# Earlier requests for w_out pieces, six buffers for turned output squares, and two queues for the third last output

## The chip, the core and the metric

The kernel runs on one NeuronCore of a Trainium2 chip. The core has a matmul engine (TensorE, PE in the profile; its weight loads are listed as PEld), VectorE (DVE), ScalarE (ACT), GpSimd (POOL) and SyncE (SP). The engines run side by side, each through its own list of instructions in a fixed order, and wait for one another through semaphores. Transfers between the memory outside (DRAM) and the memory on the chip (SBUF) are issued by an engine, here SP and, at the very end, ACT too. Results of PE land in the banks of PSUM[...].

The metric is the device time of one execution in microseconds (us), median of several runs; lower is better.

## What is computed

A causal attention with a decay for each head and without a softmax, and behind it a feed-forward layer with a squared ReLU:

```python
scores = scale * np.matmul(q, k.transpose(0, 1, 3, 2))     # q, k, v: (8, 8, 576, 64)
ret = scores * Dmat                                        # gamma[h] ** (i - j), 0 above the diagonal
attn = np.matmul(ret, v)
x = attn.transpose(0, 2, 1, 3).reshape(4608, 512)
h = np.maximum(x @ w_in, 0.0)                              # w_in: (512, 2048)
out = (h * h) @ w_out                                      # w_out: (2048, 512)
```

The two weights arrive as 64-bit floats[...]: the kernel turns them into 32-bit floats itself, by integer work on the two halves of each word.

## The kernel before

**Three stages.** The 4608 tokens are nine blocks of 512. While the attention of later tokens is computed, 128 tokens at a time, the first product (x @ w_in) of the blocks already there runs between. Then block 8's first product ends, and last comes the second product (with w_out), which runs over `N_K` = 42 outer products k, seven for each of six column sets of 384.

Both feed-forward products are made by Strassen's scheme with seven products instead of eight (`PRODUCTS`); the second uses it twice, an outer and an inner one. Block 0's first product alone is a plain one (`first_in`), since w_in is still being converted then.

**The first product, blocks 1 to 8.** `ffn_in(n, mp, j)` is one step: product j of 0 to 6 in group mp of 0 to 3 of block n. In the loop around it, `whole(i)` does the attention of 128 tokens, `loads(i)` asks for coming q, k and v, and `ffn(i - 1)` runs seven steps: a group of seven products follows every attention part. The products of a group go to three PSUM banks: h_a (j = 0 and 3), h_b (1, 4 and 6), h_c (2 and 5). Product 0 is copied by ACT (L727), 1 and 2 are added to that by DVE (L729, L731), 3 goes through ACT (L733, squared at L735), and 4, 5 and 6 are added by DVE (L736, L740, L743), each with a squaring behind it (L724). A product that adds into a bank waits until the reading of the one before it has ended. In block 1, steps 1 to 4 of the first three groups also make the four sums of w_in for the group that follows (`sum_w_in`, L257 to L260). ACT copies the running attention state out of PSUM at L503 (u_sb <- u_ps); PE's L570 adds to u_ps again.

**Converting w_out beside it.** `w_out_parts` is a generator of small actions on DVE. For each of 16 pieces: L227 (exponent bits), L231 with ACT's L235 beside it, L238, L241 and L244; after every second piece the sums of w_out (L264 to L267), and now and then a store of finished parts. A piece is asked for by `fetch_w` (L214), in four transfers on SP. The first three are actions of the generator; the others are put into the list `transfers` when the buffer they go to has been used up. How many actions a step takes is decided by `late_w2`, the number of actions that should have been done by now less `n_w2`, the number done: it begins after eight steps of block 1, takes an action whenever the number is above zero (two at j = 0 or 3 if it is above 1.5), and none in the steps that turn k and q for the attention (`busy`). `step()` runs one step and then issues one waiting transfer, or two where more than two wait, unless the attention is due within two steps (`QUIET`).

SP's order of work near the start of block 1 is: two stores of block 0's last squares (L691, the second waiting for ACT's square at L687), three stores of block 1's first group (L650), the loads of q, k and v (L158, L156), two more stores, the twelve transfers of the first three pieces (L214), and so on.

**The output.** The rows of a finished part are turned on DVE in squares of 32 by 32 (`leave`, L1036) into one of three buffers in `room` (`t_room`), used in turn, and stored from there by transfers of 32 partitions (L1043), each waiting for its own part. A store goes to the queues given in `queues` in turn: SP alone, except for the last two outer products, which `last_inner` sends out in five smaller parts over SP and ACT. The other outputs are put into the list `leaving` by `outer(k)` and leave one outer product later. The third last output is that of k = `N_K - 3`.

Of the kernel before, what the change touches and what calls it, by code (L numbers as in the profile page):

```python
# [41 lines left out]
def kernel(  # L42
# [33 lines left out]
    nc = tc.nc  # L76
# [12 lines left out]
    N_BLK = n_tok // TOK  # L89
# [39 lines left out]
    room = const.tile([128, 15872], F32, name="room")  # L129
# [36 lines left out]
    N_W1 = N_DF  # L166
# [9 lines left out]
    def raw_of(j):  # L176
        return raw_all[j % N_RAW] if j < N_W1 else raw_all[(j - N_W1) % 3]
# [27 lines left out]
    def fetch_w(j):  # L205
        if j < len(pieces) and wide:
            to = raw_of(j).bitcast(I64)
            if pieces[j][0] == 0:
                nc.sync.dma_start(to.rearrange("p (c f) -> p c f", c=N_DM), piece_src(j))
                return  # L210
            to = to.rearrange("p (o s b c) -> o s p b c", o=2, s=2, b=4)
            for o in range(2):
                for s in range(2):
                    nc.sync.dma_start(to[o, s], piece_src(j)[o, s])  # L214
# [53 lines left out]

    def w_out_parts():

        for j in range(N_W1, N_W1 + 3):
            yield lambda j=j: fetch_w(j)
        for j in range(N_W1 + 1, len(pieces), 2):

            assert not [t for t in transfers if t[0] == N_BLK]
            pair = [round_parts(j - 1), round_parts(j)]
            for one, two, beside, *_ in pair:
                yield one
                yield two, beside
            for i, (_, _, _, three, four, five) in zip((j - 1, j), pair):  # L280
                yield three
                yield four

                def last(i=i, five=five):
                    five()
                    transfers.append((N_BLK, lambda: fetch_w(i + 3)))

                yield last
            wi, m, e = pieces[j]
            mh, mq = divmod(m, N_MQ)  # L290
            if e == 1:

                at = slice(2 * mh, 2 * mh + 2)
                b = [stage[0][:, o, at, :] for o in range(4)] + [stage[1][:, o, at, :] for o in range(3)]
                r1, r2, r3, r4 = right_sums(*b)
                yield from (r1, r2, r3, r4)
            if e == 1 and mh == 1:

                def keep(o):
                    nc.sync.dma_start(w2_dram[o, :, mq, :], stage[o // 4][:, o % 4, :, :].rearrange("p s f -> p (s f)"))  # L300

                yield from right_sums(*(stage[0][:, :, o, :] for o in range(NP)))
                for o, r in enumerate(right_sums(*(stage[1][:, :, o, :] for o in range(NP)))):
                    yield lambda o=o, r=r: [r(), keep(o)]
                yield [lambda: [keep(4), keep(5)]]
                yield [lambda: keep(6)]
# [48 lines left out]
    for half in range(2):  # L355
        at = slice(CH * half, CH * half + CH)
# [345 lines left out]
    def ffn_in(n, mp, j):  # L702

        if j == 0 and mp == 0:

            if n not in sums_x:
                sums_x[n] = sum_x(n)
            for f in sums_x[n]:
                f()
        left, right, to = PRODUCTS[j]  # L710
        if j in OPENS:
            sums[to] = ps_f.tile([128, 2, HT], F32, tag="f", name=f"h_{to}")
        p = sums[to]
        for mm in range(2):
            w = w_in[mp][:, mm, WI_SLOT[left], :, :]
            for c in range(2):
                nc.tensor.matmul(p[:, mm, :], lhsT=w[:, c, :], rhs=xs[n][right][:, c, :],  # L717
                                 start=(j in OPENS and mm == 0 and c == 0), stop=(j in CLOSES and c == 1),
                                 skip_group_check=True)
        g = g_of(mp)  # L720
        p1, u2, p15 = (p_room[mp % 2][:, s, :, :] for s in range(3))

        def square(t):
            nc.vector.scalar_tensor_tensor(t, t, 0.0, t, op0=ALU.max, op1=ALU.mult)  # L724

        if j == 0:
            nc.scalar.copy(p1, p)  # L727
        elif j == 1:
            nc.vector.tensor_tensor(u2, p, p1, op=ALU.add)  # L729
        elif j == 2:  # L730
            nc.vector.tensor_tensor(p15, p, p1, op=ALU.add)  # L731
        elif j == 3:
            nc.scalar.activation(g["A11"], p, AF.Relu)  # L733
        elif j == 4:
            nc.scalar.activation(g["A11"], g["A11"], AF.Square)  # L735
            nc.vector.tensor_tensor(g["A22"], p, p15, op=ALU.add)  # L736
            square(g["A22"])
        elif j == 5:

            nc.vector.tensor_tensor(g["S3"], p, u2, op=ALU.add)  # L740
            square(g["S3"])
        else:
            nc.vector.tensor_tensor(g["A12"], p, p1, op=ALU.add)  # L743
            square(g["A12"])
            queue.extend(g_sums(n, mp))

        if j == 5:
            g_store(n, mp, "A11")
            transfers.append((n, lambda: g_store(n, mp, "A22")))

        if mp == N_MP - 1 and j in (3, 4, 5) and n_next[0] > n + 1:
            if n + 1 not in sums_x:
                sums_x[n + 1] = sum_x(n + 1)
            sums_x[n + 1].pop(0)()
        if j in (6, 0, 1, 2, 3):
            some(2 if n == 1 and mp == 0 else 1)
        if n == 1 and 1 <= j < 5 and mp + 1 < N_MP:
            sums_w.setdefault(mp + 1, sum_w_in(mp + 1)).pop(0)()

        late_w2 = 0.96 * (done[0] - N_0 - 8) - n_w2[0]  # L760
        count = 0 if busy[0] else 2 if late_w2 > 1.5 and j in (0, 3) else late_w2 > 0
        while w_out_next[0] and (count or type(w_out_next[0]) is list):
            f = w_out_next[0]
            if held[0] and type(f) is tuple or ahead[0] <= QUIET and type(f) is list:
                break
            n_w2[0] += 1
            count -= type(f) is not list
            w_out_next[0] = next(w_out_steps, None)
            for f in f if type(f) in (tuple, list) else (f,):
                f()  # L770
            if type(w_out_next[0]) is list:
                break
        if n == N_BLK - 2 and mp == 3 and j in (0, 3):
            assert w_out_next[0] is None
            fetch_w2(j // 3)

    steps = []
    w_out_steps = w_out_parts()  # L780
    w_out_next = [next(w_out_steps)]
    held = [False]
    ahead = [N_DF]
    transfers = []
    busy = [False]
    n_w2 = [0]

# [21 lines left out]
    N_0 = N_W1  # L809
    done = [0]  # L810
# [130 lines left out]
    TC = 3 * HT // 2  # L941
    NQ = TC // 2
    N_K = N_BLK * HT // TC * NP
# [3 lines left out]
    A_room = [late.tile([128, size], F32, name=f"a{j}") for j in range(2)] + [room[:, at:at + size] for at in (5888, 11776)]  # L947
    s_room = [late.tile([128, N_M * NQ], F32, name="s0"), room[:, 10240:10240 + N_M * NQ]]
    O_ = [room[:, at:at + 2 * TC].rearrange("p (e t) -> p e t", e=2) for at in (0, 2 * TC, 4 * TC)]
    t_room = [room[:, at:at + 2 * TC].rearrange("p (a e c) -> p a e c", e=2, c=32) for at in (2304, 3072, 3840)]  # L950
    LOW, HIGH = slice(0, N_MQ), slice(N_MQ, N_M)
    LEFT, RIGHT = slice(0, NQ), slice(NQ, TC)

# [70 lines left out]
    leaving = []  # L1024
    n_left = [0]
# [4 lines left out]

    def leave(k, o, h, e, es, lo, hi, queues=(nc.sync,)):

        t = t_room[n_left[0] % 3]
        n_left[0] += 1
        to, at = t[:, 0:(hi - lo) // 32, es, :], o[:, es, lo:hi]
        nc.vector.transpose(to.rearrange("p a e c -> p e a c"), at.rearrange("p e (a c) -> p e a c", c=32))  # L1036
        for b, at, c, w in runs(k // NP, lo, hi):
            row = b * TOK + h * HT + at
            to = out[row:row + w, e * HT:(e + 1) * HT].rearrange("(a r) (p e c) -> p r a e c", r=32, e=2, c=32)[:, :, :, es, :]
            lo_ = (c - lo) // 32  # L1040
            for p in range(4):
                own = slice(32 * p, 32 * p + 32)
                queues[p % len(queues)].dma_start(to[p], t[own, lo_:lo_ + w // 32, es, :])  # L1043
# [61 lines left out]
    def outer(k):  # L1105

        n, j = divmod(k, NP)
        r = state.pop(k)["r"]
        if k >= N_K - 2:
            return  # L1110
        X, Y, Z = XYZ(k)
        for to, x, with_ in {2: [(Z, r, X), (Y, Y, Z)], 3: [(X, r, X)], 4: [(Z, r, Z), (X, r, Y)], 5: [(Z, r, Z)],
                             6: [(Y, r, Y)]}.get(j, []):
            nc.vector.tensor_tensor(to, x, with_, op=ALU.add)
        if j >= 3:
            o, h, e = {3: (X, 0, 0), 4: (X, 1, 1), 5: (Z, 1, 0), 6: (Y, 0, 1)}[j]
            leaving.append(lambda: leave(k, o, h, e, slice(0, 2), 0, TC))


    n_last = 0  # L1120
# [17 lines left out]
    for k in range(N_K + 1):  # L1138
        j = k % NP
# [81 lines left out]
```

## Time and profile before

| | us |
|---|---|
| median of three runs | 937.07 (936.6 to 937.17) |
| the profiled execution, whole | 939.68 |
| its span, from the first to the last instruction | 937.6 |
| mean granted clock of PE | 0.995 |

The profile comes from one execution. Busy times are shares of its span; a timeline gives for each instruction its start, its length, engine, line, operation, result and operands, and in brackets how long the engine had stood idle and what ended that. The granted clock is the share of PE's full clock that the throttle let through in a stretch.

PE's busy share and granted clock in 40 equal slices of the span:

```profile
PE   8999989999999999999999999999999999999997
...
PEclk9999989999999999999999999999999999999999
```

### The profile page before, as it was taken

How to read it: one execution, taken by the hardware profiler on the slowest of the kernel's cores; microseconds unless marked ns; L12 is line 12 of the kernel's file. 1: busy time of each engine (PE TensorE's matmuls, PEld its weight loads, DVE VectorE, ACT ScalarE, POOL GpSimd, SP SyncE). 2: the span in 40 equal slices, each digit the busy share in tenths (PEclk: the TensorE clock that was granted, in tenths of full speed). 3: DMA queues.
4: the chain of work that ended last, by engine and by line, in shares of the span. 5: the costliest groups of instructions: out<-in, count | busy, mean ns of one | idle time of the engine just before them, and what ended most of it. 6: DMA issues, size and time to landing. Idle time of an engine off the chain costs nothing.

```text
span 937.6 us, 21090 instructions
## 1 busy us (share of the span) xinstructions
PE 925.9 (99%) x8548; PEld 832.7 (89%) x8548; DVE 760.3 (81%) x1215; ACT 346.0 (37%) x788; POOL 80.3 (9%) x82
## 2 busy tenths in 40 slices
PE   8999989999999999999999999999999999999997
PEld 7654878888888888888888899999999999999997
DVE  5888779888888798888866587888788888877876
ACT  3457756676676766766721110000000000000000
POOL 3222011211211111111000000000000000000000
PEclk9999989999999999999999999999999999999999
DMA  9998376667766776675369997566666575465523
GB/s 224 212 256 236 100 194 181 192 187 252 197 173 212 237 195 189 176 256 170 114 247 346 375 326 213 143 157 192 171 175 193 151 209 155 115 182 139 158 66 68
DMA packets 297376, 181.29 MB, mean 193 GB/s; under 512 B 194368, under 2 KB 270272, under 8 KB 296384
## 3 DMA queue, kind: packets, MB, share of 16 engines
q1 hardware_dynamic: 293040, 179.04, 66.1%
q8 instruction: 67, 1.10, 0.5%
q10 hardware_dynamic: 4240, 0.92, 0.5%
q14 instruction: 29, 0.24, 0.1%
HBM read 109.39 MB, written 70.52 MB: 192 GB/s over the span
## 4 chain that ended last, share of the span: by engine, by line
PE 97%; DMA 1%; DVE 1%; issue 0%; SPq 0%; ACTq 0%; DVEq 0%
PE h_b L717 18%; PE o_b L1058 17%; PE h_a L717 13%; PE h_c L717 12%; PE o_a L1058 12%; PE o_c L1058 11%; PE h_ps L679 6%; PE x_ps L576 3%; PE sc_ps L482 2%; PE x_ps L611 1%; PE u_ps L570 1%; DMA q_ld<-in_q_dram 1%; DMA out_dram<-room 1%; PE t_ps L447 0%; PE sc_ps L511 0%
## 5 line engine op out<-in xcount | busy, mean ns | idle before, releaser
L717 PE MATMUL h_b<-room,w 128*128 128x256 f32 x768 | 182.0, 380 | 0.0
L433 ACT COPY qk<-flip 32x256 f32<-32x256 f32 x432 | 173.8, 402 | 6.7
L717 PEld LDWEIGHTS h_b<-room,w 128*128 128x128 f32 x768 | 146.4, 191 | 20.2
L717 PE MATMUL h_a<-room,w 128*128 128x256 f32 x512 | 125.7, 389 | 0.0
L717 PE MATMUL h_c<-room,w 128*128 128x256 f32 x512 | 121.0, 379 | 0.0
L717 PEld LDWEIGHTS h_c<-room,w 128*128 128x128 f32 x512 | 97.3, 190 | 13.2
L717 PEld LDWEIGHTS h_a<-room,w 128*128 128x128 f32 x512 | 96.0, 192 | 14.1
L1058 PE MATMUL o_b<-room,w 128*128 128x192 f32 x496 | 90.7, 326 | 0.0
L1071 ACT COPY r<-o_a 128x192 f32<-128x192 f32 x28 | 8.9, 318 | 209.4 <-PE o_a L1058 209.4
L1058 PEld LDWEIGHTS o_b<-room,w 128*128 128x128 f32 x496 | 82.3, 190 | 0.0
L724 DVE SCALAR_TENSOR_TENSOR room<-room 128x512 f32<-128x512 f32 x96 | 68.3, 711 | 3.3
L398 POOL TENSOR_TENSOR q_ld<-q_ld,dv 128x512 f32<-128x512 f32 x34 | 37.8, 1110 | 291.7 <-DMA q_ld<-in_q_dram 236.7
L1058 PE MATMUL o_a<-a,w 128*128 128x192 f32 x352 | 62.6, 326 | 0.0
L1058 PE MATMUL o_b<-s,w 128*128 128x192 f32 x336 | 61.5, 326 | 0.0
L1058 PE MATMUL o_c<-s,w 128*128 128x192 f32 x336 | 61.5, 326 | 0.0
L1058 PE MATMUL o_c<-room,w 128*128 128x192 f32 x336 | 61.5, 326 | 0.0
L679 PE MATMUL h_ps<-room,w 128*128 128x512 f32 (+1 forms) x152 | 57.7, 532 | 0.6 <-DVE w L244 0.5
L1058 PEld LDWEIGHTS o_a<-a,w 128*128 128x128 f32 x352 | 58.1, 190 | 0.1
L1058 PE MATMUL o_a<-room,w 128*128 128x192 f32 x320 | 56.9, 326 | 0.0
L1058 PEld LDWEIGHTS o_b<-s,w 128*128 128x128 f32 x336 | 55.8, 190 | 0.0
L1058 PEld LDWEIGHTS o_c<-s,w 128*128 128x128 f32 x336 | 55.8, 190 | 0.0
L1058 PEld LDWEIGHTS o_c<-room,w 128*128 128x128 f32 x336 | 55.8, 190 | 0.0
(116 smaller groups left out, 1414.2 us busy)
## 6 DMA issues: line engine op xcount, KB each, us to landing
g_dram<-room SPq DMA_DIRECT2D x164, 256.0 KB, 3.8
a<-g_dram SPq DMA_DIRECT2D x30, 512.0 KB, 5.8
room<-g_dram SPq DMA_DIRECT2D x28, 512.0 KB, 5.1
w_dram<-w SPq DMA_DIRECT2D x28, 448.0 KB, 5.0
w<-w_dram SPq DMA_DIRECT2D x7, 1792.0 KB, 9.9
q_ld<-in_q_dram SPq DMA_DIRECT2D x64, 128.0 KB, 3.8
w<-in_moe_w_in_dram SPq DMA_DIRECT2D x16, 512.0 KB, 6.8
w<-in_moe_w_out_dram SPq DMA_DIRECT2D x64, 128.0 KB, 3.6
```

Source lines behind the costliest of these rows:

```text
L398: engine.tensor_tensor(t, t, dv[:, heads, at:at + 1].to_broadcast(list(t.shape)), op=ALU.mult)
L433: nc.scalar.copy(*moves.pop(0)[2:])
L482: nc.tensor.matmul(st[i]["sc"][e][rows(h), hp, :], lhsT=st[i]["kT"][rows(e), hp, t], rhs=st[i]["qT"][rows(e), hp, t], start=True, stop=Tru ...
L570: return [lambda hp=hp, e=e, b=b: nc.tensor.matmul(u[rows(e), hp, :], lhsT=loaded[i][1][rows(h), 2 * hp + e, :], rhs=st[i]["vs"][rows(h), ...
L576: return [lambda hp=hp, e=e, b=b: nc.tensor.matmul(x_at(hp, e, b, h), lhsT=s["vs"][rows(h), head(hp, e), :], rhs=s["ret"][rows(h), e, hp, ...
L611: m = nc.tensor.matmul(x_at(hp, e, b, h), lhsT=u[rows(e), hp, :], rhs=s["qT"][rows(e), hp, CH * h:CH * h + CH], start=clears(b, e), stop=F ...
L679: nc.tensor.matmul(p, lhsT=w[:, c, :], rhs=xT[0][:, c, :].rearrange("p (h t) -> p h t", h=2)[:, lo:hi, at[0]:at[1]], start=(c == 0), stop= ...
L717: nc.tensor.matmul(p[:, mm, :], lhsT=w[:, c, :], rhs=xs[n][right][:, c, :], start=(j in OPENS and mm == 0 and c == 0), stop=(j in CLOSES a ...
L724: nc.vector.scalar_tensor_tensor(t, t, 0.0, t, op0=ALU.max, op1=ALU.mult)
L1058: nc.tensor.matmul(p, lhsT=w_out[j][:, m, WO_SLOT[right], :], rhs=s["lefts"][left][:, m, :], start=(i in OPENS and m == 0), stop=(i in CLO ...
L1071: nc.scalar.copy(r[:, 0, LEFT], p)
```

## The change

Three edits go together.

1. The first three pieces of w_out are no longer fetched by actions of the generator. At the first step of block 1 (n = 1, mp = 0, j = 0) their requests are put into `transfers`, from which `step()` issues them. Since the three no longer count among the actions, the rate goes from 0.96 to 0.94 of an action per step.
2. `t_room` has six buffers instead of three.
3. The third last output is stored over SP and ACT in turn instead of over SP alone.

```diff
     def w_out_parts():
 
-        for j in range(N_W1, N_W1 + 3):
-            yield lambda j=j: fetch_w(j)
         for j in range(N_W1 + 1, len(pieces), 2):
...
         if j == 0 and mp == 0:
 
+            if n == 1:
+                transfers.extend((N_BLK, lambda i=i: fetch_w(i)) for i in range(N_W1, N_W1 + 3))
             if n not in sums_x:
...
-        late_w2 = 0.96 * (done[0] - N_0 - 8) - n_w2[0]
+        late_w2 = 0.94 * (done[0] - N_0 - 8) - n_w2[0]
...
-    t_room = [room[:, at:at + 2 * TC].rearrange("p (a e c) -> p a e c", e=2, c=32) for at in (2304, 3072, 3840)]
+    t_room = [room[:, at:at + 2 * TC].rearrange("p (a e c) -> p a e c", e=2, c=32) for at in (2304, 3072, 3840, 4608, 8960, 14848)]
...
-        t = t_room[n_left[0] % 3]
+        t = t_room[n_left[0] % len(t_room)]
...
-            leaving.append(lambda: leave(k, o, h, e, slice(0, 2), 0, TC))
+            leaving.append(lambda: leave(k, o, h, e, slice(0, 2), 0, TC, (nc.sync, nc.scalar) if k == N_K - 3 else (nc.sync,)))
```

The order of PE's instructions stays the same. DVE's conversion of w_out comes a few steps earlier in block 1, and SP's twelve transfers of L214 stand right behind the two stores of L691.

More of the change, by code (lines that the diff above doesn't have):

```diff
@@ L765, in ffn_in @@
                 break
+            assert n_w2[0] or not [t for t in transfers if t[0] == N_BLK]
             n_w2[0] += 1
@@ L779 @@
     steps = []
+    transfers = []
     w_out_steps = w_out_parts()
@@ L783 @@
     ahead = [N_DF]
-    transfers = []
     busy = [False]
```

## The prediction

> **What bounds the kernel now.** I read the page's busy shares and its chain first, then the waits of the matmul engine (PE), then the chain in order of time for places where its rhythm breaks, and last the timelines of VectorE (DVE), ScalarE (ACT) and SyncE (SP) around the two places found.
>
> From the page, parts 1 and 4, and the list of PE's waits between 26 and 925 us:
>
> ```profile
> PE 925.9 (99%) x8548; PEld 832.7 (89%) x8548; DVE 760.3 (81%) x1215; ACT 346.0 (37%) x788; POOL 80.3 (9%) x82
> ...
> PE 97%; DMA 1%; DVE 1%; issue 0%; SPq 0%; ACTq 0%; DVEq 0%
> ```
>
> ```profile
> PE u_ps L570 <- issue: 2.7, 1, 2.7
> ```
>
> PE is the bound, and between 26 and 925 us it stands still once. The change leaves its instructions and their order alone. So there are three questions: what the one stall costs in all, what happens behind the last matmul, and whether the reordered DVE makes PE wait anew.
>
> The chain in order of time (start, length) shows the price of the stall. A group (seven products of L717 with their attention work) begins at each h_a x8 of 1.92 us:
>
> ```profile
> 95.53 1.92 PE h_a L717 x8
> ...
> 109.89 1.93 PE h_a L717 x8
> ...
> 123.61 2.69 issue
> 127.85 3.71 PE h_a L717 x8
> 131.56 2.21 PE h_b L717 x8
> ...
> 158.80 1.93 PE h_a L717 x8
> ...
> 216.25 1.93 PE h_a L717 x8
> ```
>
> Block 1's four groups take 158.80 - 95.53 = 63.27 us, the four after them 216.25 - 158.80 = 57.45. Block 1 loses 5.82 us, and only 2.69 of it is the stall: the next eight h_a take 3.71 us for 1.92. The windows (length, busy times of PE, PEld, DVE, ACT, POOL, granted clock, DMA share, GB/s) say why:
>
> ```profile
> 109.90:123.60 13.70, 13.70 (x140) 11.85 (x140) 9.50 (x12) 9.07 (x21) 2.11 (x2) 1.00 0.69 178
> 123.60:126.30 2.70, 0.01 (x2) 0.03 (x1) 1.51 (x3) 0.98 (x2) 0.00 (x0) 0.87 0.98 216
> 125.50:132.40 6.90, 6.10 (x55) 5.12 (x56) 5.96 (x11) 3.43 (x9) 0.00 (x0) 0.51 0.88 223
> ```
>
> PE worked 6.10 us at half clock, so half of that, 3.05, is lost: 2.69 + 3.05 = 5.74, within 0.1 of the 5.82 counted.
>
> Who causes the stall stands in the timelines of DVE and ACT:
>
> ```profile
> 124.76 0.43 DVE L227 TENSOR_SCALAR w<-w 128x512 uint32<-128x512 uint32 x1 [3.09 <-DMA w<-in_moe_w_out_dram]
> ```
>
> ```profile
> 125.22 0.72 ACT L235 ACTIVATE w<-w,exp_bias 128x512 uint32<-128x512 uint32 x1 [5.26 <-DVE w L227]
> 125.85 0.35 ACT L503 COPY u_sb<-u_ps 128x256 f32<-128x256 f32 x1
> ```
>
> The first w_out piece lands late (SP issues the twelve parts of three pieces from 118.2 to 127.0). L227 waits for it, L235 for L227, and behind L235 in ACT's order sits L503, which empties u_ps. It ends at 126.20, and PE's L570 starts at 126.30.
>
> The tail, from DVE's timeline:
>
> ```profile
> 931.09 0.58 DVE L1036 STREAM_TRANSPOSE room<-room 128x384 f32<-128x384 f32 x1 [0.66 <-DMA out_dram<-room]
> 931.59 0.32 DVE L1095 TENSOR_TENSOR room<-o_b,small 128x192 f32<-128x192 f32 x1
> 932.92 0.38 DVE L1036 STREAM_TRANSPOSE room<-room 128x192 f32<-128x192 f32 x1 [1.01 <-DMA out_dram<-room]
> ```
>
> PE ends at 931.33. The last two transposes wait for the stores of the turned squares three uses earlier.
>
> [...] Here L258 took 1.53 and L260 1.57 us for 0.68 elsewhere, each beside a POOL product (115.84 and 120.06). [...] In the tail an issue takes 0.43 us median on SP and 0.44 on ACT, and landing 1.7: there issue time counts.
>
> **The change part by part.**
>
> *Fetches at the first step of block 1.* The twelve issues move from step 10 on to steps 1 and 2. On SP they stand directly behind L691, whose second issue waits for the squares of L687 (97.99 + 0.63 = 98.6). Twelve issues at 8.80 / 12 = 0.73 us run from 99.0 to 107.8, and with 3.6 us to landing the last piece is there at 111.4. Behind them wait three stores of L650 (from 104.78 before): about 3 us later, and their buffers are written again only two groups, 28 us, on. The third of them waits for L656's sum at 109.9 anyway, so the loads of q, k and v behind it stay at 110.3. The loads of the next group, held to 128.6 by the old burst, come about 2 us sooner. Conversion starts at step 10 with L227 itself, near 117.5, 6 us behind the landing. The 5.82 us go, with the three waits that made them.
>
> *0.94 for 0.96.* Fetches no longer count, so 152 actions remain for 155: 0.94 x 161 = 151, 0.96 x 161 = 155. The end stays where it was, and the start runs up to three actions ahead. I give it nothing by itself. Its risk is the next part.
>
> *What is late next: DVE in group 3 of block 1.* Groups 1 to 3 also carry four sums of w_in each (L257 to L260). The changed order puts L227, L231, L227, L231, L238, L241 into group 2. Walking it with start distances from the timeline (0.61 for a sum of 512, 0.34 for L227 and L231, 0.72 and 0.61 for an addition with its square, L258 at 1.53 beside POOL as before), L736 starts at 119.1, L740 at 122.0, L743 at 123.9, and after L241, L493 and two transposes group 3's L729 at 128.9. Its product ends at 124.25 + 1.93 + 1.73 = 127.9: DVE is 0.95 late. From L729 to L736 the kernel before took 133.87 to 139.68 with 0.37 idle, so 5.44 of work with one POOL collision: L736 starts at 134.34 and has read its bank 0.65 later, at 135.0. The seventh product, which adds into that bank, is due at 127.9 + 4 x 1.73 = 134.8. That is a new stall of 0.2 us; a second collision (the POOL products now fall near 131 and 133.5) makes it 0.85, none makes it nothing. I take 0.5. Group 4 has no sums of w_in, and DVE catches up. A stall of half a microsecond inside full products should not cost the clock (PE waits of 0.3 to 0.5 us before 95 us left it at 1.00).
>
> *Six buffers.* 27 squares leave; the last three would reuse buffers whose stores landed before 922. The two waits (0.66 and 1.01) go. The last transpose follows the last addition: PE end 931.33, L1095 at 931.37 for 0.32, L1036 931.73 to 932.11, against 932.92 to 933.29. The rows at 4608, 8960 and 14848 lie clear of the operands in that stage, so no other wait is traded for it.
>
> *Third last output on two queues.* SP loses four of its last 22 issues, ACT gains four on 14. With both free at 924.0, an issue every 0.45 us and at most eight transfers in flight (each semaphore waits for its previous transfer), the eight stores of the third last output end at 925.8, the next eight at 927.6; four from 928.55, four from 929.57, eight from 931.09, and the last four from 932.87 with the last starting at 933.3. The profile before has its last issue at 934.93 and its landing at 936.50, 1.57 later. So the last landing moves to 934.9: 1.6 us, for both tail edits together. From below it is 0 (eight in flight already the limit), from above 2.0[...].
>
> **Sum.** 5.82 - 0.5 + 1.6 = 6.9 us. The profiled run took 939.68, of it 937.6 in the span and 2.08 around it; it would become 932.8. The median shown is 937.07, 2.6 under the profiled run; the same 6.9 gives **930.2**.
>
> **The rivals.**
> *The clock drop belongs to the profiled run alone.* The profiled run is 2.6 over the median, near the 3.05 of the drop[...]. Then 2.69 - 0.2 + 1.6 = 4.1: 932.9.
> *Eight in flight is the tail's limit.* SP's semaphore wait until 930.66 speaks for it, ACT's idle gaps against. Then 5.3 alone: 931.8.
> *The fetch does not come early enough.* If the burst stays blocked on SP until 114, L227 waits as before and only the tail gains: 935.5. The 6 us of slack speak against it.
> *The tail gives nothing and the stall only moves:* 937.
> *DVE becomes the bound while w_out is converted (slower).* Its place is L736 before the seventh product, with 0.31 us of slack in group 3 before (read until 140.36, product at 140.67). If the actions that run ahead make it miss in each of the 23 groups that convert, 0.5 us each is 11.5 - 6.9 = 4.6 more: 941.7. From 0.3 per group on it is slower. Against it: the other groups lack the sums of w_in, PE waited in none of them, and the new rate is the lower one.
>
> **How the numbers follow.** Forecast 0.60 (own range 929.2 to 931.2), clock drop only profiled 0.20, tail limited 0.08, fetch still late 0.05, nothing 0.03, DVE the bound 0.04. Within 0.2% (1.9 us) a measurement here cannot be told from no change. Faster: 0.60 + 0.20 + 0.08 + 0.05 = 0.93; same 0.03; slower 0.04. The range reaches from 928.9 (no stall in group 3, tail 2.0) to 933.2 (the second case with 0.5 lost in group 3).
>
> **What would show it.** Right: no wait of L227 for a DMA, no PE "issue" of 2.7 us, block 1's four groups within 58.2 us, no half clock after 10 us; L736 of group 3 ending near 135; no L1036 waiting for a DMA, span end about 4.7 us after PE's last matmul rather than 6.3. Wrong: a PE wait over 1 us in block 1, a granted clock under 1.00 there, new short PE waits in blocks 2 to 7, or a tail that stays at 6.3.

## The result and the profile after

| | before | after |
|---|---|---|
| median, us | 937.17 (936.6 to 939.24, 5 runs) | 933.2 (932.86 to 933.57, 5 runs) |
| the profiled execution | 939.68 | 933.57 |
| its span | 937.6 | 931.9 |
| block 1's four groups | 63.27 | 58.62 |
| the four groups after them | 57.45 | 57.46 |
| PE's last matmul to the end of the span | 6.27 | 5.05 |

The ratio is 0.9951 (0.9937 to 0.9966): the change makes the kernel about 4 us faster. The two profiled executions lie 6.1 us apart, the medians 4.0. That difference is the first thing to explain.

The chain of the changed kernel in order of time (start, length), at the first product of the groups:

```profile
95.65 1.92 PE h_a L717 x8
...
110.01 1.93 PE h_a L717 x8
...
139.97 1.92 PE h_a L717 x8
...
154.27 1.93 PE h_a L717 x8
...
211.73 1.92 PE h_a L717 x8
```

154.27 - 95.65 is 58.62 us; 211.73 - 154.27 is 57.46. Block 1 still loses 1.2 us, where it lost 5.8. Where it loses them stands in PE's waits between 26 and 925 us:

```profile
PE h_b L717 <- DVE room L736: 1.0, 1, 1.0
```

and in DVE's timeline of the third group (start, length, line):

```profile
128.90 0.65 DVE L729 TENSOR_TENSOR room<-h_b,room 128x512 f32<-128x512 f32 x1
129.47 0.67 DVE L257 TENSOR_TENSOR w<-w 128x512 f32<-128x512 f32 x1
130.06 0.68 DVE L731 TENSOR_TENSOR room<-h_c,room 128x512 f32<-128x512 f32 x1
130.66 1.18 DVE L258 TENSOR_TENSOR w<-w 128x512 f32<-128x512 f32 x1
131.76 0.68 DVE L244 SCALAR_TENSOR_TENSOR w<-w,w 128x512 uint32<-128x512 uint32 x1
132.37 0.68 DVE L259 TENSOR_TENSOR w<-w 128x512 f32<-128x512 f32 x1
132.97 1.54 DVE L238 SCALAR_TENSOR_TENSOR w<-w,w 128x512 f32<-128x512 uint32 x1
134.54 0.69 DVE L241 SCALAR_TENSOR_TENSOR w<-w,w 128x512 f32<-128x512 f32 x1
135.15 0.68 DVE L736 TENSOR_TENSOR room<-h_b,room 128x512 f32<-128x512 f32 x1
```

There is no bracket in these lines: DVE never stood idle, it is simply late. Two of the instructions were stretched, L258 to 1.18 and L238 to 1.54 (0.68 each where POOL stands idle), and POOL's timeline shows its two products beside them:

```profile
130.23 1.06 POOL L396 TENSOR_TENSOR q_ld<-q_ld,dv 128x512 f32<-128x512 f32 x1 [9.02 <-DVE w L257]
132.78 1.18 POOL L495 TENSOR_TENSOR v_ld<-v_ld,dv 128x512 f32<-128x512 f32 x1 [1.49 <-DMA v_ld<-in_v_dram]
```

L736 ends at 135.83, and the seventh product of the group, due at 134.8, starts behind it, at 135.89. No instruction of L227 waits for a piece of w_out any more. The clock in block 1 (length, busy PE, PEld, DVE, ACT, POOL, granted clock, DMA share, GB/s):

```profile
95.50:154.30 58.80, 57.84 (x715) 50.18 (x707) 52.26 (x83) 40.30 (x92) 6.92 (x7) 1.00 0.64 171
```

In the tail the last two transposes start right behind the additions (DVE's timeline; line numbers of kernel.py are one higher here than in the kernel before, so L1036 is L1037):

```profile
925.54 0.36 DVE L1096 TENSOR_TENSOR room<-o_c,small 128x192 f32<-128x192 f32 x1 [0.53 <-PE o_c L1059]
925.93 0.58 DVE L1037 STREAM_TRANSPOSE room<-room 128x384 f32<-128x384 f32 x1
926.84 0.36 DVE L1096 TENSOR_TENSOR room<-o_b,small 128x192 f32<-128x192 f32 x1 [0.33 <-PE o_b L1059]
927.25 0.38 DVE L1037 STREAM_TRANSPOSE room<-room 128x192 f32<-128x192 f32 x1
```

and both queues carry the same load, 18 issues each, where SP had 22 and ACT 14:

```profile
919.48 10.13 SPq L1044 DMA_DIRECT2D out_dram<-room  x18
...
919.48 9.87 ACTq L1044 DMA_DIRECT2D out_dram<-room  x18
```

### The profile page after: what moved, and what is told of

The parts are those of the page before. It is cut to its first block, busy times and chain, and to the rows that moved or that the text cites. A ratio compares the mean times of both kernels' runs of the same rounds, so it can differ in the third digit from the quotient of the medians.

```text
span 931.9 us, 21078 instructions
## 1 busy us (share of the span) xinstructions
PE 922.2 (99%) x8548; PEld 830.0 (89%) x8548; DVE 756.4 (81%) x1215; ACT 346.3 (37%) x788; POOL 82.1 (9%) x82
## 4 chain that ended last, share of the span: by engine, by line
PE 96%; DVE 2%; DMA 1%; ACT 0%; issue 0%; SPq 0%; DVEq 0%
PE h_b L717 17%; PE o_b L1059 17%; PE h_a L717 12%; PE o_c L1059 12%; PE o_a L1059 12%; PE h_c L717 11%; PE h_ps L677 6%; PE x_ps L574 3%; PE sc_ps L480 2%; PE x_ps L609 1%; PE u_ps L568 1%; DMA k_ld<-in_k_dram 1%; PE t_ps L445 0%; PE sc_ps L509 0%; PE x_ps L535 0%; DVE w L238 0%
```

## The experiments

Ten kernels ran, each with a profile of its own and 5 to 22 runs, between runs of the kernel before: 42 of these beside the first four kernels (median 938.35), 17 beside the next four (937.87), 9 beside the last two (938.29). The numbers come first, in one table, since several readings draw on more than one row. The first column of times is the median with the lowest and highest run; the ratio, with a 95% interval, is taken from the runs of both kernels and is not exactly the quotient of the two medians; the other columns are read from the one profiled execution: block 1's four groups, the length of the stretch at half clock that begins in block 1, PE's wait for L736, and the tail from PE's last matmul to the end of the span.

| kernel | us | ratio to before | four groups | half clock | L736 | tail |
|---|---|---|---|---|---|---|
| before, profile of the start | 937.17 | | 63.27 | 6.83 | 0 | 6.27 |
| before_again | 938.40 (936.24 to 940.63) | 1.0004 (0.9993 to 1.0015) | 62.44 | 3.41 | 0 | 6.28 |
| fetch | 934.75 (934.07 to 936.12) | 0.9966 (0.9956 to 0.9977) | 58.54 | 0 | 0.9 | 6.28 |
| tail | 935.75 (934.45 to 938.62) | 0.9978 (0.9969 to 0.9987) | 62.93 | 3.41 | 0 | 5.03 |
| same_order | 932.72 (932.47 to 933.13) | 0.9946 (0.9930 to 0.9963) | 58.00 | 0 | 0.3 | 5.04 |
| after_again | 933.43 (932.98 to 933.99) | 0.9958 (0.9946 to 0.9971) | 58.74 | 0 | 1.1 | 5.03 |
| six | 941.72 (939.98 to 943.03) | 1.0042 (1.0028 to 1.0056) | 63.88 | 6.83 | 0 | 9.36 |
| two | 936.20 (934.84 to 939.03) | 0.9990 (0.9980 to 1.0000) | 61.27 | 0 | 0.7 | 5.04 |
| start14 | 932.61 (932.02 to 933.61) | 0.9951 (0.9938 to 0.9963) | 57.40 | 0 | 0 | 5.05 |
| after_three | 932.45 (932.25 to 933.57) | 0.9939 (0.9927 to 0.9952) | 58.25 | 0 | 0.6 | 5.03 |
| start14_three | 932.23 (932.07 to 932.60) | 0.9935 (0.9921 to 0.9948) | 57.58 | 0 | 0 | 5.04 |

From the first product of block 2 to PE's last matmul every one of these traces takes 772.5 to 772.9 us. Nearly all of the difference in the spans is in the four groups, in the tail, and before the first group, which starts between 95.03 and 96.02.

**before_again: the kernel before, unchanged.**

> The kernel before, unchanged, to see whether the clock drop behind its one stall is the same in every run. Theory A (the drop differs from run to run[...]): times spread over 2 us or more (936.5 to 939.5), and a lower granted clock goes with a longer time: about 0.995 where two windows are lost, 0.997 where one is, 0.998 where none is. Rival B (the drop belongs to the profiled run alone): all other runs at 0.998 and within 0.6 us of 937.

The times spread over 4.4 us, and this profile shows another drop than the first one did. Two stretches around the stall of 2.9 us:

```profile
122.90:126.30 3.40, 0.47 (x27) 0.36 (x22) 1.62 (x3) 0.98 (x2) 0.00 (x0) 1.00 1.09 218
126.80:130.30 3.50, 3.50 (x27) 2.75 (x19) 3.46 (x7) 1.95 (x5) 0.00 (x0) 0.51 0.97 261
```

The half clock lasts 3.41 us here and 6.83 in the first profile; the expectations call these one window and two. Of the 68 runs of the kernel before beside the experiments, 33 have a mean granted clock of 0.998 or more and a median of 936.96 us, 26 have 0.996 or less and 939.1, and the nine between 938.4. (The sorting is not clean: in the first profile half clock comes again from 934.54 us on, behind the last matmul, which ends at 931.33, and it lowers the mean without making any matmul longer.) The time before is a mixture: the stall is there in all five traces of kernels that fetch late, and the drop behind it is of 6.83 us, 3.41 us, or missing. Theory A holds. The drop is not all that varies: ten of the 33 runs with the higher clock took 938.07 to 938.88 us, and what they lose is not known.

The missing drop can be read from the profile of `two`, the kernel with the second queue alone, with the clock at 1.00 in the stall of 2.7 us and behind it:

```profile
123.40:126.30 2.90, 0.25 (x13) 0.19 (x12) 1.66 (x4) 0.98 (x2) 0.00 (x0) 1.00 1.11 222
126.30:132.00 5.70, 5.70 (x67) 5.06 (x64) 5.67 (x12) 4.81 (x12) 0.00 (x0) 1.00 0.80 211
```

The length of the stall does not order the drops:

| kernel | PE's stall, us | half clock behind it, us |
|---|---|---|
| before | 2.7 | 6.83 |
| two | 2.7 | 0 |
| before_again | 2.9 | 3.41 |
| six | 2.9 | 6.83 |
| tail | 3.3 | 3.41 |

In the first profile PE was not idle throughout the 3.42 us before the drop, nor in the first half of the half clock:

```profile
122.16:125.58 3.42, 1.45 (x85) 1.31 (x84) 0.82 (x2) 0.36 (x1) 0.00 (x0) 1.00 1.00 223
125.58:128.99 3.41, 2.69 (x47) 2.42 (x48) 3.34 (x7) 1.87 (x6) 0.00 (x0) 0.50 0.95 241
```

What decides which of the three comes is not shown. In the first two traces the stretches between two changes of the clock are 119.47, 6.83 and 802.13 us long (the kernel before) and 925.01 (the changed one): 35, 2, 235 and 271 times 3.413.

**fetch: the early fetch and the rate 0.94 alone.**

```diff
-        for j in range(N_W1, N_W1 + 3):
-            yield lambda j=j: fetch_w(j)
...
+            if n == 1:
+                transfers.extend((N_BLK, lambda i=i: fetch_w(i)) for i in range(N_W1, N_W1 + 3))
...
-        late_w2 = 0.96 * (done[0] - N_0 - 8) - n_w2[0]
+        late_w2 = 0.94 * (done[0] - N_0 - 8) - n_w2[0]
```

> The early fetch with the rate 0.94 alone, tail as before. Theory A: the tail gave 1.2 us and the new wait of L736 takes 1.0, so this has 933.2 + 1.2 = 934.4, 2.8 less than before's 937.2, and no spread above 1 us. Rival B (the tail gave more than the profile's 1.2, up to 2.0, and block 1 less): 935.2.

934.75 against 934.4 and 935.2: in between, and the profile decides for A: the tail is before's to a hundredth, 6.28, and block 1 takes 58.54 us with a wait of 0.9 for L736, near the 1.0 of the whole change. The stall and the drop are gone. `same_order`, further down, fetches early too but converts in the order of the kernel before, and has no stall either: it is the fetch that removes it, not the new rate. The spread is 2.05 us, twice what A allowed, without any half clock in the profile before the last matmul; where those runs lose time was not followed up.

**tail: six buffers and two queues alone.**

```diff
-    for at in (2304, 3072, 3840)]
+    for at in (2304, 3072, 3840, 4608, 8960, 14848)]
...
-        t = t_room[n_left[0] % 3]
+        t = t_room[n_left[0] % len(t_room)]
...
-            leaving.append(lambda: leave(k, o, h, e, slice(0, 2), 0, TC))
+            leaving.append(lambda: leave(k, o, h, e, slice(0, 2), 0, TC, (nc.sync, nc.scalar) if k == N_K - 3 else (nc.sync,)))
```

> Six buffers and two queues alone, fetch as before. Theory A: 1.2 us less than before, 936.0 where the drop is small and up to 938.3 where it is whole, with before's spread. Rival B: 935.2 to 935.5. In the profile the span ends 5.1 us behind PE's last matmul instead of 6.3, and the stall of 2.7 us is still there.

The stall is still there, 3.3 us long. The tail is 5.03 us for 6.27: 1.24. In the times it is 0.9978, 2.1 us with an interval of 1.2 to 2.9, at whose lower edge the profile's number lies. The medians of two mixtures differ by more or less than what was changed, depending on how many runs of each had the drop; the tail read from the profile does not have that fault.

**two and six: the parts of the tail one by one.**

> The second queue alone, three buffers; fetch as before. Theory A: with four issues fewer ahead of them on SP, the stores that free the buffers land about 1.8 us sooner, so the two waits for buffers shrink or go as well: 0.8 to 1.2 us off the tail, span end 5.1 to 5.5 us behind PE's last matmul. Rival B: the waits for buffers stay at 1.7 and the tail gains nothing, 6.3 behind.

> Six buffers alone; fetch and queues as before. Theory A (SP's string of issues holds the tail as well as the buffers do): the transposes no longer wait for a DMA, but SP issues to nearly the same time: 0.3 to 0.7 us off the tail, span end 5.6 to 6.0 us behind PE's last matmul. Rival B (the buffers alone held the tail): 1.2 us, 5.1 behind.

The second queue alone takes the tail to 5.04 us, the whole gain, and the two waits of L1036 for a DMA are gone with three buffers as well: the stores that free the buffers were late only because they stood behind SP's string. This is theory A, by the profile; in the times the ratio of 0.9990 has an interval that reaches 1.0000, so there the gain is not clear of no change. Six buffers alone make the kernel *slower*, by 0.42% (0.28 to 0.56), 3.9 us, which neither theory had. The tail accounts for 3.1 of them. DVE no longer waits for a DMA, and yet the tail is 9.36 us long. SP's own waits from 915 us on, first with three buffers, then with six:

```profile
SPq L1043 <- DMA out_dram<-room: 1.0, 1, 1.0
```

```profile
SPq L1043 <- DMA out_dram<-room: 4.6, 4, 2.7
```

and its timeline in the kernel with six buffers:

```profile
926.89 4.74 SPq L1043 DMA_DIRECT2D out_dram<-room  x4
```

SP gets four issues out in 4.74 us, which take 0.43 each in the median of the kernel before. ACT meanwhile gets its last eleven out from 926.86 to 934.44, and SP, which still has 14 to make at 931.31, works them off one after another until 939.08: its issuing ends 4.64 us behind ACT's, for 0.90 in the kernel before (935.37 and 934.47). That ACT's stores ran ahead with six buffers and so held SP's back is the author's estimate: whose transfers SP waited for is not shown by these views.

**same_order and start14: what makes PE wait for L736.** The first leaves the conversion's actions where the kernel before had them, so that DVE's instructions come in before's order; the second begins the conversion six steps later. Against the changed kernel:

```diff
-        late_w2 = 0.94 * (done[0] - N_0 - 8) - n_w2[0]
+        late_w2 = 0.96 * (done[0] - N_0 - 8) - n_w2[0] - 3
```

```diff
-        late_w2 = 0.94 * (done[0] - N_0 - 8) - n_w2[0]
+        late_w2 = 0.94 * (done[0] - N_0 - 14) - n_w2[0]
```

> All of the change, but with the conversion's actions at the steps they had before (rate 0.96, three actions later), so that DVE's order is that of the kernel before. Theory A (the 1.0 us wait of PE for L736 in block 1's third group comes from the conversion running ahead): that wait falls to 0.3 or nothing, 932.3, 0.9 less than the changed kernel. Rival B (the wait comes from POOL's products meeting DVE, wherever the conversion stands): the wait stays at 0.7 to 1.0 and the time at 933.2.

> The changed kernel with the conversion beginning six steps later (after 14 steps of block 1 for 8), so that DVE comes into the third group of block 1 with less behind it. Theory A (the conversion running ahead makes DVE late at L736): PE's wait there is gone, block 1's four groups take 57.5 to 57.8 us for 58.6, and the time is 0.9 to 1.1 us under the changed kernel's, 932.2. Rival B (the later conversion only moves the lateness into the fourth group or to the end of block 7): 933 or more, with PE waiting in another place.

In before's order the wait is 0.3 us, and PE's only other wait after 26 us is 0.3 in the attention. DVE's timeline shows that POOL meets it twice here too (L258 took 1.21 us, L241 1.43) and that L736 starts at 134.72, 0.43 sooner than in the changed kernel, though the groups began 0.2 later. Both theories have a share. The wait itself differs from one execution to the next: the four profiles with the changed kernel's block 1 (the changed kernel twice, `fetch` and `after_three`) have 1.0, 1.1, 0.9 and 0.6. Against the 0.3 here, 0.3 to 0.8 us come from the actions that run ahead. That the rest comes from POOL's products is argued from the stretched sums, not tested. Before's own profile had no such wait: the products at half clock gave DVE 2.3 us more (3.71 and 2.21 for 1.92 and 1.73), and it stood idle for 2.34 before L729. L736 was hidden by the loss that the change removes. The kernel with the second queue alone fits this from the other side. In its profiled run the drop did not come, and PE waits twice:

```profile
PE u_ps L570 <- issue: 2.7, 1, 2.7
PE h_b L717 <- DVE room L736: 0.7, 1, 0.7
```

With the later start DVE comes to L729 of the third group with 1.36 us to spare, one of the short actions takes 1.28 us for 0.42, and L736 still ends at 134.01, 0.8 us before the seventh product needs its bank:

```profile
127.99 0.69 DVE L729 TENSOR_TENSOR room<-h_b,room 128x512 f32<-128x512 f32 x1 [1.36 <-PE h_b L717]
...
132.12 1.28 DVE L227 TENSOR_SCALAR w<-w 128x512 uint32<-128x512 uint32 x1
133.33 0.68 DVE L736 TENSOR_TENSOR room<-h_b,room 128x512 f32<-128x512 f32 x1
```

Block 1's groups take 57.40 us, no more than the groups after them; theory A's place is right. The time is 932.61, 0.4 above what A gave: 0.4 us came back between block 2 and the last matmul (772.9 for 772.5). By the times alone this kernel and the changed one, 933.43 in the same series, are not clearly apart; their runs overlap (932.02 to 933.61, 932.98 to 933.99).

**after_again: the changed kernel beside them.**

> The changed kernel, unchanged, beside the others. Theory A (before's time is a mixture, since the clock drop behind its stall is lost in some runs and not in others; the changed kernel has no drop): 932.8 to 933.8 in every run, granted clock 0.998 or more, and the distance to before is 4 us where before's runs have lost little clock and 6 to 7 where they lost two windows. Rival B (the changed kernel has such a mixture too): a spread of 2 us or more.

932.98 to 933.99 in five runs, granted clock 0.998 to 1.0, no half clock in the profile before the last matmul: the mixture is gone along with the stall.

**after_three and start14_three: without the six buffers.** The changed kernel, and the one with the later start, each with the three buffers of before.

> The changed kernel with its three buffers for turned squares instead of six. Theory A (the second queue gives the whole gain of the tail, the six buffers none): 933.4, within 0.5 us of the changed kernel, span end 5.0 to 5.1 us behind PE's last matmul. Rival B (each edit gives part of it): 933.9 to 934.3, a wait of L1036 for a DMA comes back.

> The same with the conversion beginning after 14 steps: early fetch, later conversion, second queue, three buffers. Theory A: like the kernel with six buffers and this start, 932.6 (932.0 to 933.3), no wait of PE between 26 us and its last matmul. Rival B: 933.1 or more.

Both tails are those of six buffers (5.03 and 5.04), no L1037 waits for a DMA, and the times are not higher; after_three is even 0.95 us below the 933.4 that A gave, more than the 0.5 allowed, and start14_three 0.4 below its 932.6. No gain of the six buffers shows once the second queue is there. The lowest median of the study is that of start14_three, at 0.9935 (0.9921 to 0.9948): the early fetch, the later start of the conversion, the second queue, and three buffers. Its PE waits for nothing from 26 us to its last matmul. Against the changed kernel the gain is about 1 us in the profile's parts; in the times the runs of the two kernels do not overlap (932.07 to 932.60; 932.86 to 933.99 over its ten runs), but they were measured in different series. In its own series after_three has 932.25 to 933.57, which does overlap: by the times the later start is not shown to be faster.

## Why the prediction was right in direction and 3 us too low

- *The stall, its chain and its cure: right.* L227 waited for the fetch, L235 for L227, L503 behind it, PE for L503. With the fetch alone all of it is gone, and block 1's groups fall from 62.4 to 63.9 us (61.3 where no drop came) to 58.5. SP's burst ran from 99.19 to 108.20, for 99.0 to 107.8 forecast, and the stores and loads behind it cost nothing.
- *The step that failed is the sum's last one: "the same 6.9 gives 930.2".* The sum was made against the profiled run of 939.68, which had the whole drop, 6.83 us of half clock, and then taken from the median of 937.07. Runs at that level are those that lost little or no clock (936.96 is the median of the 33 with the higher clock). Between the two profiled executions 6.1 us were gained, between the medians 4.0. (The clock of those first runs is not among the numbers here; that they are of the better kind is concluded from their times.) What block 1 costs without the drop can be estimated from the trace of `two`, whose block 1 is that of the kernel before: 61.27 us. The drop adds 2.0 to that, not the 3.05 of the lost clock, because without it DVE is late at L736 for 0.7. Then 61.27 - 58.62 = 2.65 in block 1, 1.22 in the tail, less 0.12 before the first group, and 0.4 around the span make 4.15, close to the 4.0 measured. The prediction had this as its first rival, at 0.20, put as a drop that belongs to the profiled run alone (932.9). The rival's size was nearly right, its wording not: by the clocks the drop comes in something like half of all runs (35 of the 68 have a mean clock below 0.998). The three runs before lay within 0.6 us of each other; 68 runs lie within 4.7.
- *DVE late at L736: right place, half the size.* Taken at 0.5, bounded at 0.85 for two meetings with POOL; there were two, and it was 1.0 us, 1.2 with what else block 1 loses. L729 was forecast at 128.9 and started at 128.90; L736 was forecast at 134.34, which a second meeting (0.85 - 0.2 = 0.65) moves to 135.0, and started at 135.15. The 5.44 us of work between them were taken over from the kernel before, where the short L231 (0.41) stood in that place; in the new order it is L244 (0.68).
- *The tail: 1.2 us for 1.6.* In the walk the eight stores of the last but one part were issued from 931.09 and the last four from 932.87, 1.78 us; in the trace it is 926.54 to 928.48 and 928.80, 1.94 to 2.26, since SP waits once more for a transfer of ACT's to land: its issue of 928.80 uses the semaphore of the one that ACT issued at 926.96, which landed at 928.74. The eight in flight that the walk counts with are in the traces of both kernels: the 836 transfers of SP and ACT carry eight semaphores between them, and there are never more than eight between issue and landing. So such a wait for an earlier transfer, which the rival of eight in flight (0.08) stands for, took a share.
- *"For both tail edits together": the prediction didn't part them, and one of them does harm alone.* It explained the gain by the six buffers first. The second queue gives all of it.
- *0.94 for 0.96 at nothing by itself: nothing speaks against it.* Blocks 2 to 8 and the second product take the same 772.5 us before and after, and `same_order` with 0.96 takes them too. The rate alone was not run.
- *Slips in the sums.* With no stall in the third group and 2.0 in the tail the lower end is 937.07 - 7.82 = 929.25, not 928.9. The first rival's 937.07 - 4.1 is 933.0, not 932.9, and with 0.5 lost in the third group it is 933.3, not 933.2. None of them bears on the reasoning.
- The sum against the profile, part by part: 63.27 - 58.62 = 4.65 in block 1, 1.22 in the tail, less 0.12 lost before the first group, is 5.75, the 5.7 of the spans; 0.4 more lay around the span.

## What to carry to other kernels

A stall with half clock behind it can cost a different amount in each run (here 6.83 us of half clock, 3.41 or none); a sum made against one profiled run must be set against a median of runs that may not have paid it, and the granted clock of each run helps to tell which they are. Where a large wait goes, look for the work that used its time to catch up: it is late next, and here a later start of the displaced work took that wait away. Where buffers seem to hold the end of a kernel, ask first what keeps their transfers from being issued: splitting a string of issues over two queues freed the buffers too, and more buffers without it made the end longer, with one queue done 4.64 us ahead of the other.

## What had not been expected of the hardware

- A stall of 2.7 to 3.3 us at the same place of the program led to no half clock, to 3.41 us of it, or to 6.83, in five traces. With a stall of 2.7 us there was one trace with 6.83 and one with none.
- A DVE action with one input was stretched beside a POOL product as the sums with two inputs are: in `same_order` L227 took 1.28 us at 121.00, with POOL's product of 1.24 at 120.76 beside it, and 0.42 at 125.79, with none. The forecast had counted such meetings for the sums only.
- Six buffers for three, with nothing else changed, lengthened the tail by 3.1 us (9.36 for 6.28).
